# A convolution and an MLP on one core: five first-product blocks placed ahead of second products behind octet blocks, and five forward-1 blocks moved to even half steps

## The chip, the cores and the metric

The kernel runs on one core of a Trainium2 chip. The metric is the device time of one execution in microseconds. Five engines matter: TensorE (PE, matrix products; PEld is its weight load), VectorE (DVE), ScalarE (ACT), GpSimd (POOL) and SyncE (SP, which here only issues DMAs). Each engine works through its own queue in the order in which the program was written, and they wait for each other by semaphores.

## What is computed

Cut to what matters (x is `A_q`, 2048 rows of 448; F is 1792):

```python
xn = layernorm(x)
k_shift = sum of four shifted copies of k, each times its tap     # depthwise conv, 4 taps
kv = k_shift * v
y = causal convolution of kv with ssm_k over 2048 rows, by FFT    # per channel
y = y + kv * ssm_D
h = xn @ w1 + b1
out = x + xn * y + (h * tanh(softplus(h))) @ w2
```

## The kernel before, in words

The MLP is the spine. The 2048 rows are 8 chunks of 256, and the 1792 hidden columns are 14 blocks of 128, taken two at a time: 7 pairs per chunk, 56 pairs in all, numbered i. The loop at the end of `tile_kernel` runs over half steps s, two for each pair. Function `mlp_slot` says what a half step holds:

- even half step s = 2i: the first product of pair i (`g1_mm`, 22 matmuls of 256 columns, line L555), which is h for 256 columns of w1, held as a high and a low part;
- odd half step s = 2i + 1: Mish of pair i (`mish`: ACT activations L563, ACT cast of the high part `ach` L97, DVE subtraction for the low part `acl` L98), and then the second product of pair i - 2 (`g2_mm`, 12 matmuls of 448 columns, lines L587 to L589).

A chunk's second products gather in two PSUM tiles (`pg2`, one for each half of 128 rows). The pool has two buffers, so the next chunk's first second product can't begin until DVE has added both to the rows of x (`g2_evac`, line L594, output `qt`). For chunk c this addition is written at the head of the even half step behind the chunk's last second product; for chunk 2 alone (`EVAC_SOON`) it stands directly behind that product.

The convolution is hung into the same loop by two tables of work per half step, `plan` (ahead of the MLP's part, filled by `at`) and `plan2` (behind it, filled by `after`). Its stages:

- Half steps up to 62: forward-1 blocks. Each of 8 groups of the filter (`h`, half steps `H_AT`) and 8 groups of kv (half steps `KV_AT`) gets one block `f1_mm` (L165) of tiles of 32 rows by 64 columns, written to PSUM tiles `pq` and `pr`. `f1_fold` empties them: ACT copies one (L171), DVE adds and subtracts (L175) into a staging tile `st` with two buffers. `f1_out` (L186) sends `st` to DRAM (`Dh`, `Dkv`), from ACT's queue for all that matters here. Ahead of a kv block stand its taps (`taps`, DVE lines L208, L211, L213, L218, L221, result `x`; one of the four taps is multiplied by POOL, L201). If a block stands at half step t and the one before it at t - d, tap u is written behind half step t - 2 - d + d * u / 4, rounded down.
- Half steps 66 to 87, every third: octets (`octet`): inverse-1 of the octet before (`i1_mm`, L309), then two forward-2 blocks (`f2_mm`, L254), of the filter part `ah` and of the kv part `av`, loaded from DRAM by `o_load` (L238, L241). Even half steps hold an octet and then a first product; odd ones hold an octet and then a second product. The first product behind an odd octet goes to PSUM bank `pa`, which the octet itself has used.
- After half step 92: inverse-2 and the gate.

So at an odd half step with a forward-1 block, PE's row is first product, forward-1, second product, first product; at an even one it is second product, forward-1, first product, second product.

Of the kernel before, what the change touches and what calls it, by code (L numbers as in the profile page):

```python
# [20 lines left out]
NO = 8  # L21
# [1 line left out]

G2_LAG = 2
H_HEAD = 1
H_AT = {2: 6, 3: 9, 0: 12, 4: 16, 5: 20, 6: 26, 7: 32}
KV_AT = (24, 29, 34, 39, 44, 50, 55, 59)
POOL_H = {20: (0, 2)}
OCT_AT = (66, 3)
I2_AT = {100: ((6, 7, 0, 1), 92, (95, 97, 98, 99), (0, 2, 0, 1)),  # L30
# [9 lines left out]
NT_HOW[5] = dict(NT_AT, q=-8, stats=-4, flush=-2)  # L40
NT_STATS = {3: 27, 4: 41, 5: 53, 6: 70, 7: 82}
EVAC_SOON = 2,
END = 288
HEAD = (D, D, 192 + NF, 512, 2 * D, 512)
WARM_N = (448, 448, 448)
# [4 lines left out]
def tile_kernel(ctx: ExitStack, tc, q, qT, k, v, sk, hT, sD, head, w1, w2, c_g, c_gi, c_i2, out):  # L50
# [24 lines left out]
    Dh = dp.tile([NO * 16, 32, D], F32, name="Dh")  # L75
    Dkv = dp.tile([NO * 16, 32, D], F32, name="Dkv")
# [19 lines left out]
    def split(h, l, raw):  # L96
        nc.scalar.copy(h, raw)  # L97
        V.tensor_sub(l, raw, h)  # L98
# [7 lines left out]
    def bank(n):  # L106
        return bk(duo[n // 2], n % 2)

    def pg():
        return g1p[0].tile([128, 512], F32, name="pg1")  # L110
# [9 lines left out]
    def dv(n=1):  # L120
        for _ in range(n):
            if drip:
                drip.pop(0)()
# [4 lines left out]
    def at(slot, fn, *args):  # L128
        plan.setdefault(int(slot), []).append((fn, args))
# [97 lines left out]
    GT, AH, AV, HS, Y = {}, {}, {}, {}, {}  # L227
# [172 lines left out]
    def w1_hi(p, a=0, b=256):  # L400
        nc.scalar.copy(w1h[:, :, 256 * p + a:256 * p + b], w1_raw(p, a, b))

    def w1_lo(p, a=0, b=256, eng=V):
        fs, rw = slice(256 * p + a, 256 * p + b), w1_raw(p, a, b)
        V.tensor_sub(w1l[:, :, fs], rw[:, 0:3], w1h[:, 0:3, fs])
        eng.tensor_sub(w1h[64:128, 3, fs], rw[64:128, 3], w1h[64:128, 3, fs])
# [128 lines left out]
    def g1_mm(i):  # L535
        c, p = pairs[i]
        XH, XL = XS[c]
        pt = [(bank(GB[i]) if i in GB else pg()).rearrange("p (a b) -> p a b", a=2) for _ in range(2 if i == 0 else 1)]
        ps = [pt[n % len(pt)][:, n] for n in range(2)]
        mm = [[], []]  # L540
        for n in range(2):
            f = 2 * p + n
            fs = slice(128 * f, 128 * f + 128)
            hh, hl, lh = ([(w[:, kt, fs], x[:, kt]) for kt in range(3)] for w, x in ((w1h, XH), (w1h, XL), (w1l, XH)))
            th, tl = ((w1h[:, 3, fs], x[:, 3]) for x in (XH, XL))
            mm[n] = [(n, *m) for m in hh + lh + [th] + hl + [tl]]

            if 0 < i < NP:
                mm[n] = [(n, *m) for m in hh + hl + lh + [th, tl]]
        if i == 0:  # L550
            seq = mm[0][:7] + mm[1][:3] + mm[0][7:] + mm[1][7:10] + mm[1][3:7] + mm[1][10:]
        else:
            seq = mm[0] + mm[1]
        for n_, (n, l, r) in enumerate(seq):
            nc.tensor.matmul(ps[n], l, r, start=all(m[0] != n for m in seq[:n_]), stop=all(m[0] != n for m in seq[n_ + 1:]))  # L555
        P1[i] = ps

    def mish(i):
        p = pairs[i][1]
        ps = P1.pop(i)  # L560
        a = mp.tile([128, 2, CH], F32, name="a", bufs=2)
        for n in range(2):
            nc.scalar.activation(a[:, n], ps[n], AF.Mish, bias=b1t[:, 2 * p + n:2 * p + n + 1])  # L563
            if i == n == 0:
                w1_hi(2)
        if i == 0:
            w1_lo(2)
        ah = mp.tile([128, 2, CH], F32R, name="ach", bufs=3)
        al = mp.tile([128, 2, CH], F32R, name="acl", bufs=3)
        AHL[i] = ah, al  # L570
        if 2 * i + 1 in hv:
            held.append(lambda: split(ah, al, a))
        else:
            split(ah, al, a)
            dv()
# [15 lines left out]
    def g2_evac(c, jjs=(0, 1)):  # L591
        x = Q[c]
        for jj in jjs:
            V.tensor_add(x[:, jj], P2.pop((c, jj))[:, :D], x[:, jj])  # L594
            dv()
            if late(c):
                nc.sync.dma_start(out[:, 2 * c + jj], x[:, jj])

    def g2_end(j):
# [4 lines left out]
        g2_evac(c, (0,))  # L604
        for b, cs, eng in ((0, slice(0, END), nc.scalar), (2, slice(END, D), nc.sync)):
            ps = bank(b)[:, :cs.stop - cs.start]
# [9 lines left out]
    def mlp_slot(s):  # L616
        i, half = divmod(s, 2)
        n = len(pairs)
        j = i - G2_LAG
        if half == 0:  # L620
            if i < n:
                c, p = pairs[i]
                if c + 1 < NT:
                    if p == 0:
                        ln_load(c + 1)
                    if p == (3 if c in (0, 2) else 2):
                        ln_stats(c + 1)
                    if c == 0:
                        dv(len(drip))
                    if p == NP - 1:  # L630
                        ln_T(c + 1, 1)
                g1_mm(i)
        else:
            if i < n:
                c, p = pairs[i]
                if p == NP - 2 and c + 1 < NT:
                    ln_T(c + 1, 0)
                if s not in hv:
                    mish(i)
            if 0 <= j < n - 1:  # L640
                g2_mm(j)
                if pairs[j][1] == NP - 1 and pairs[j][0] in EVAC_SOON:
                    g2_evac(pairs[j][0])
            elif j == n - 1:
                g2_end(j)
# [4 lines left out]

    for g, t in H_AT.items():
        if g != H_HEAD:
# [10 lines left out]
    for g in range(-2, 0):  # L663
        at(12, k_load, g)
    for g, t in enumerate(KV_AT):
        d = t - (KV_AT[g - 1] if g else t - 6)
        at(t - d - (3 if g > 1 else 2), k_load, g)
        at(t - d - 1, v_load, g)
        for u in range(4):
            after(t - (2 if g else 1) - d + d * u / 4, taps, g, u)  # L670
        at(t, f1_mm, KV, g, "kv")
        if g + 1 < NO:
            after(t, taps_pool, g + 1, 2)
        after(t, f1_fold, g, "kv")
        (at if t % 2 else after)(t + (3 if g < NO - 1 else 2), f1_out, Dkv, g, "kv")

    for p in range(NP):
        if p >= 3:
# [11 lines left out]
    for o in range(NO):  # L690
        s, d = OCT_AT[0] + OCT_AT[1] * o, OCT_AT[1]
        ib, hb, vb = ((0, 1), (2, 0), (1, 2)) if s % 2 == 0 else ((0, 2), (1, 0), (2, 1))
        (at if o else after)(s - d if o else s - 7, o_load, AH, Dh, o, "ah")
        at(s - d - 1 if o else s - 3, o_load, AV, Dkv, o, "av")
        at(s, octet, o, ib, hb, vb)
        at(s, gi_load, o)
        after(s, prod, o)
        if s % 2:
            hv.add(s)
            GB[s // 2 + 1] = 0  # L700
        else:
            GB[s // 2], GB[s // 2 + 1] = 0, 2
# [100 lines left out]
    for s in range(nslots):  # L803
        j = s // 2 - G2_LAG - 1
        if s % 2 == 0 and j >= 0 and pairs[j][1] == NP - 1 and pairs[j][0] not in EVAC_SOON:
            g2_evac(pairs[j][0])
# [85 lines left out]
```

## Time and profile before

| what | value |
|---|---|
| median of 3 runs | 356.9 us (356.87 to 358.35) |
| the profiled execution | 357.13 us, of which the span from first to last instruction is 355.4 |
| granted TensorE clock, mean | 0.999 |
| DVE busy | 282.8 us, 80% of the span |
| ACT, POOL busy | 160.4 us (45%), 73.7 us (21%) |

The page's second part cuts the span into 40 slices of 8.9 us, a digit for each: the busy share in tenths. The row of DVE:

```profile
DVE  5999658998999998997539868868985963788943
```

DVE is nearly full from about 62 to 160 us (the eighth digit to the eighteenth): there the taps and folds of the kv blocks lie.

### The profile page before, as it was taken

What the parts mean: (1) busy time and instruction counts of PE and PEld (TensorE: products, weight loads), DVE (VectorE), ACT (ScalarE), POOL (GpSimd) and SP (SyncE); (2) the same over time, 40 slices, a digit from 0 to 9 for tenths busy, and PEclk for the clock granted to TensorE, in tenths of its full rate; (3) what the DMA queues carried; (4) which work ended last, traced back from release to release, by engine and by line L of the source; (5) the groups of instructions that cost most, each with busy time, mean ns of one, the idle gap of its engine ahead of it and who ended that gap; (6) DMA issues with size and microseconds to landing.
All of it is one profiled execution on the core that took longest, in us unless ns stands there. A gap on an engine that the chain in (4) does not pass through costs nothing.

```text
span 355.4 us, 7520 instructions
## 1 busy us (share of the span) xinstructions
PE 351.0 (99%) x3098; PEld 290.2 (82%) x3098; DVE 282.8 (80%) x375; ACT 160.4 (45%) x310; POOL 73.7 (21%) x85
## 2 busy tenths in 40 slices
PE   8999999999999999999999999999999999999996
PEld 3988888888888989888987568658757799979795
DVE  5999658998999998997539868868985963788943
ACT  4966552347343643373232732233634333354480
POOL 3047002822220250222000120110310116040030
PEclk9999999999999999999999999999999999999999
DMA  7999977949769347664869489679755466989176
GB/s 262 370 328 321 410 291 175 344 121 245 207 182 315 126 149 177 216 162 110 245 198 352 122 310 314 224 237 378 252 183 210 105 170 258 406 332 277 28 116 144
DMA packets 30835, 83.27 MB, mean 234 GB/s; under 512 B 3153, under 2 KB 15954, under 8 KB 30802
## 3 DMA queue, kind: packets, MB, share of 16 engines
q1 hardware_dynamic: 21986, 47.78, 39.5%
q0 software_dynamic: 4928, 22.95, 20.7%
q10 hardware_dynamic: 3888, 12.08, 13.1%
q8 instruction: 24, 0.39, 0.4%
q14 instruction: 9, 0.07, 0.1%
HBM read 54.34 MB, written 28.45 MB: 233 GB/s over the span
## 4 chain that ended last, share of the span: by engine, by line
PE 99%; DVE 0%; issue 0%
PE pg L555 24%; PE pg L587 13%; PE pg L589 13%; PE pg L588 12%; PE pa L555 6%; PE pq L555 5%; PE pq L165 4%; PE pa L309 3%; PE pr L555 3%; PE pq L254 3%; PE pr L254 3%; PE pp L555 2%; PE pa L254 1%; PE pg L743 1%; PE pp L363 1%; PE pg L507 1%
## 5 line engine op out<-in xcount | busy, mean ns | idle before, releaser
L587 PE MATMUL pg<-w2h,ach 128*128 128x448 f32 x222 | 81.7, 368 | 0.0
L589 PE MATMUL pg<-w2h,acl 128*128 128x448 f32 x222 | 80.7, 364 | 0.0
L588 PE MATMUL pg<-w2l,ach 128*128 128x448 f32 x222 | 80.5, 363 | 0.0
L98 DVE TENSOR_TENSOR acl<-a,ach 128x512 fp32r<-128x512 f32 x56 | 38.9, 695 | 34.3 <-ACT ach L97 34.2
L555 PE MATMUL pg<-XH,w1h 128*128 128x256 f32 x264 | 52.7, 283 | 0.0
L563 ACT ACTIVATE a<-pg,b1t 128x256 f32<-128x256 f32 x66 | 27.8, 471 | 54.3 <-PE pg L555 43.4
L587 PEld LDWEIGHTS pg<-w2h,ach 128*128 128x128 f32 x222 | 41.6, 188 | 9.4 <-issue 5.0
L555 PEld LDWEIGHTS pg<-XH,w1h 128*128 128x128 f32 x264 | 41.5, 188 | 6.8 <-issue 4.2
L589 PEld LDWEIGHTS pg<-w2h,acl 128*128 128x128 f32 x222 | 41.7, 188 | 2.5
L588 PEld LDWEIGHTS pg<-w2l,ach 128*128 128x128 f32 x222 | 41.8, 188 | 2.3
L555 PE MATMUL pg<-XL,w1h 128*128 128x256 f32 x264 | 43.0, 278 | 0.0
L175 DVE TENSOR_TENSOR st<-pq,st 128x896 f32<-128x896 f32 x32 | 34.8, 1089 | 4.7 <-ACT st L171 3.8
L555 PEld LDWEIGHTS pg<-XL,w1h 128*128 128x128 f32 x264 | 36.0, 188 | 0.0
L97 ACT CAST ach<-a 128x512 fp32r<-128x512 f32 x56 | 34.8, 621 | 1.7
L555 PE MATMUL pg<-XH,w1l 128*128 128x256 f32 x198 | 33.6, 279 | 0.0
L201 POOL TENSOR_TENSOR x<-kr,skb 128x896 f32<-128x896 f32 x8 | 17.0, 2128 | 70.5 <-PE pr L165 26.3
L320 POOL DMA_DIRECT2D E<-qe x14 | 8.8, 630 | 94.4 <-ACT qe L263 94.4
L218 DVE TENSOR_TENSOR x<-x 128x896 f32<-128x896 f32 x24 | 26.2, 1092 | 2.0 <-POOL x L201 1.4
L555 PEld LDWEIGHTS pg<-XH,w1l 128*128 128x128 f32 x198 | 27.7, 189 | 0.0
L171 ACT COPY st<-pr 128x896 f32<-128x896 f32 x16 | 14.5, 906 | 13.5 <-PE pr L165 10.7
L563 ACT ACTIVATE a<-pa,b1t 128x256 f32<-128x256 f32 x16 | 6.7, 471 | 30.5 <-PE pa L555 30.5
L165 PE MATMUL pr<-x,con 32*64 32x448 f32 x128 | 15.9, 560 | 0.0
(191 smaller groups left out, 649.2 us busy)
## 6 DMA issues: line engine op xcount, KB each, us to landing
Dkv<-st ACTq DMA_DIRECT2D x16, 448.0 KB, 5.2
ah<-Dh SPq DMA_DIRECT2D x8, 896.0 KB, 7.6
av<-Dkv SPq DMA_DIRECT2D x8, 896.0 KB, 9.5
e<-E POOLq DMA_DIRECT2D x8, 896.0 KB, 7.3
E<-qe POOLq DMA_DIRECT2D x14, 448.0 KB, 7.2
kr<-in_k_dram SPq DMA_DIRECT2D x10, 448.0 KB, 5.9
Dh<-st ACTq DMA_DIRECT2D x10, 448.0 KB, 6.8
x<-in_v_dram SPq DMA_DIRECT2D x8, 448.0 KB, 6.2
```

Of the source, the lines that this page charges most:

```text
L97: nc.scalar.copy(h, raw)
L98: V.tensor_sub(l, raw, h)
L165: nc.tensor.matmul(ps[h][64 * jj:64 * jj + 64, b, :D], f1[rg:rg + 32], x[rg:rg + 32, jj], start=True, stop=True, tile_position=(rg, 64 * jj))
L175: f(st[:, n], e, st[:, 1])
L201: nc.gpsimd.tensor_mul(o, KR[g - u // 2], skb[:, u:u + 1].to_broadcast([128, 2, D]))
L218: V.tensor_add(KV[g], KV[g], o)
L254: nc.tensor.matmul(bk(p, r)[32 * t:32 * t + 32, :D], g[rs, t, c], a[rs, t], start=True, stop=True, tile_position=(64 * r, 32 * t))
L555: nc.tensor.matmul(ps[n], l, r, start=all(m[0] != n for m in seq[:n_]), stop=all(m[0] != n for m in seq[n_ + 1:]))
L563: nc.scalar.activation(a[:, n], ps[n], AF.Mish, bias=b1t[:, 2 * p + n:2 * p + n + 1])
L587: nc.tensor.matmul(ps, ah[:, n, cs], w2h[:, f], start=f == 0, stop=False)
L588: nc.tensor.matmul(ps, ah[:, n, cs], w2l[:, f], start=False, stop=False)
L589: nc.tensor.matmul(ps, al[:, n, cs], w2h[:, f], start=False, stop=f == NF - 1 or (f == NF - 3 and jj == 1 and c == NCHUNK - 1))
```

## The change

The diff, all of it:

```diff
-H_AT = {2: 6, 3: 9, 0: 12, 4: 16, 5: 20, 6: 26, 7: 32}
-KV_AT = (24, 29, 34, 39, 44, 50, 55, 59)
+H_AT = {2: 6, 3: 10, 0: 12, 4: 16, 5: 20, 6: 26, 7: 32}
+KV_AT = (24, 30, 34, 40, 44, 50, 56, 60)
...
+G1_SOON = (69, 75, 81, 87, 89)
...
-                g1_mm(i)
+                if s - 1 not in G1_SOON:
+                    g1_mm(i)
...
                 if s not in hv:
                     mish(i)
+            if s in G1_SOON:
+                g1_mm(i + 1)
             if 0 <= j < n - 1:
                 g2_mm(j)
...
-        (at if t % 2 else after)(t + (3 if g < NO - 1 else 2), f1_out, Dkv, g, "kv")
+        (after if g < NO - 1 else at)(t + (3 if g < NO - 1 else 2), f1_out, Dkv, g, "kv")
...
-        (at if o else after)(s - d if o else s - 7, o_load, AH, Dh, o, "ah")
+        (at if o else after)(s - d if o else s - 6, o_load, AH, Dh, o, "ah")
```

It has two halves. First, at the odd half steps 69, 75, 81 and 87 (octets 1, 3, 5 and 7) and at 89 (the last inverse-1) the next pair's first product is written ahead of the second product, and is left out of the even half step behind. Second, the forward-1 blocks at 9, 29, 39, 55 and 59 go to 10, 30, 40, 56 and 60; their taps, folds and stores go with them. The distances d between kv blocks, which were 5, 5, 5, 5, 6, 5, 4, become 6, 4, 6, 4, 6, 6, 4. The first load of `ah` moves one half step later. Line numbers from 43 to 631 are one higher in the changed kernel: L98 before is L99 after, L594 is L595, L165 is L166. No instruction is added or taken away on any engine but for semaphore work.

**First place: PE around kv block 1, at half step 29 before and 30 now** (the four other blocks that move look the same). Before, from the last matmuls of pair 14's first product to the second product behind the block:

```order
L555 MATMUL pg_1052<-XL,w1h 128x256 x4
L165 MATMUL pq<-x,con 64x448 x2
L165 MATMUL pr<-x,con 64x448 x2
L165 MATMUL pq<-x,con 64x448 x2
L165 MATMUL pr<-x,con 64x448 x2
L587 MATMUL pg_753<-w2h,ach 128x448
```

And in the changed kernel, from the last matmul of the second product to the first product behind the block:

```order
L590 MATMUL pg_757<-w2h,acl 128x448
L166 MATMUL pq<-x,con 64x448 x2
L166 MATMUL pr<-x,con 64x448 x2
L166 MATMUL pq<-x,con 64x448 x2
L166 MATMUL pr<-x,con 64x448 x2
L556 MATMUL pg_1108<-XH,w1h 128x256 x3
```

The block has gone behind one second product (12 matmuls); a first product now follows it where a second product did.

**Second place: DVE between half steps 29 and 32.** Here stand the second half of the taps of kv block 2 (half step 34 in both kernels), the fold of kv block 1, and at the end the emptying of chunk 1's second products (`qt`). Before, from the low half of pair 14's Mish on:

```order
L98 TENSOR_TENSOR acl<-a,ach 128x512
L200 MEMSET x 1x1
L175 TENSOR_TENSOR st<-pq,st 128x896 x2
L218 TENSOR_TENSOR x<-x 128x896
L211 TENSOR_TENSOR x<-kr,skb 128x448
L213 TENSOR_TENSOR x<-kr,skb 128x448
L218 TENSOR_TENSOR x<-x 128x896
L221 TENSOR_TENSOR x<-x 128x896
L98 TENSOR_TENSOR acl<-a,ach 128x512
L594 TENSOR_TENSOR qt<-pg_753,qt 128x448
L594 TENSOR_TENSOR qt<-pg_757,qt 128x448
```

And in the changed kernel, directly behind the same low half of pair 14 (its own row is left out here):

```order
L212 TENSOR_TENSOR x<-kr,skb 128x448
L214 TENSOR_TENSOR x<-kr,skb 128x448
L219 TENSOR_TENSOR x<-x 128x896
L201 MEMSET x 1x1
L176 TENSOR_TENSOR st<-pq,st 128x896 x2
L219 TENSOR_TENSOR x<-x 128x896
L99 TENSOR_TENSOR acl<-a,ach 128x512
L212 TENSOR_TENSOR x<-kr,skb 128x448
L214 TENSOR_TENSOR x<-kr,skb 128x448
L219 TENSOR_TENSOR x<-x 128x896
L222 TENSOR_TENSOR x<-x 128x896
L595 TENSOR_TENSOR qt<-pg_753,qt 128x448
```

Three instructions of tap 1 (L212, L214 and the sum L219) stood ahead of that low half before and now stand behind it, so they lie between it and `qt`. Pair 15's low half still stands ahead of `qt`.

**Third place: PE behind the octet of half step 69.** Before, from the end of forward-2:

```order
L254 MATMUL pb<-ah,g 32x448
L254 MATMUL pr<-av,g 32x448 x8
L254 MATMUL pq<-av,g 32x448 x8
L587 MATMUL pg_2053<-w2h,ach 128x448
L588 MATMUL pg_2053<-w2l,ach 128x448
L589 MATMUL pg_2053<-w2h,acl 128x448
```

And in the changed kernel:

```order
L255 MATMUL pb<-ah,g 32x448
L255 MATMUL pr<-av,g 32x448 x8
L255 MATMUL pq<-av,g 32x448 x8
L556 MATMUL pa<-XH,w1h 128x256 x3
L556 MATMUL pa<-XH,w1l 128x256 x3
L556 MATMUL pa<-XH,w1h 128x256
```

The first product of pair 35 has moved ahead of the second product of pair 32; behind it two second products stand in a row.

## The prediction

> **What bounds the kernel now.** I read the page's busy times first and then its chain of waits:
>
> ```profile
> PE 351.0 (99%) x3098; PEld 290.2 (82%) x3098; DVE 282.8 (80%) x375; ACT 160.4 (45%) x310; POOL 73.7 (21%) x85
> ...
> PE 99%; DVE 0%; issue 0%
> ```
>
> PE is busy for 99% of the span and the chain that ended last runs on PE alone. The change adds and removes no matmul. So it can gain only the few hundredths of a microsecond that PE loses where one kind of block follows another, and it can lose whatever PE comes to wait for. I take the two apart: first PE's own pace, then the queues that the moved work is put into. Base is the profiled execution, 357.13 us, its span of 355.4 and 1.73 around it; it lies 0.23 us above the median of 356.9.
>
> **PE's pace around a forward-1 block.** The timeline of PE, first row of each block (start, duration, then the tile), gives block times as differences of starts:
>
> ```profile
> 97.46 0.36 PE L587 MATMUL pg<-w2h,ach 128*128 128x448 f32 x1
> ...
> 99.96 0.59 PE L165 MATMUL pq<-x,con 32*64 32x448 f32 x2
> ...
> 100.89 0.62 PE L555 MATMUL pg<-XH,w1h 128*128 128x256 f32 x3
> ...
> 103.52 0.36 PE L587 MATMUL pg<-w2h,ach 128*128 128x448 f32 x1
> ...
> 105.92 0.52 PE L555 MATMUL pg<-XH,w1h 128*128 128x256 f32 x3
> ...
> 108.42 0.36 PE L587 MATMUL pg<-w2h,ach 128*128 128x448 f32 x1
> ...
> 110.83 0.51 PE L555 MATMUL pg<-XH,w1h 128*128 128x256 f32 x3
> ...
> 113.42 0.59 PE L165 MATMUL pq<-x,con 32*64 32x448 f32 x2
> ...
> 114.36 0.47 PE L587 MATMUL pg<-w2h,ach 128*128 128x448 f32 x1
> ...
> 116.88 0.52 PE L555 MATMUL pg<-XH,w1h 128*128 128x256 f32 x3
> ...
> 119.47 0.37 PE L587 MATMUL pg<-w2h,ach 128*128 128x448 f32 x1
> ```
>
> Undisturbed, a second product takes 2.40 us (103.52 to 105.92) and a first product 2.50 (105.92 to 108.42). Around the even block at 99.96 the second product takes 2.50, the block 0.93 and the first product 2.63: 6.06 for the three. With one undisturbed first product (2.50) that is 8.56. The odd block at 113.42 holds the same four blocks, first product, forward-1, second product, first product, from 110.83 to 119.47: 8.64. What is dearer is the last one: the first product behind the second product takes 2.59 instead of 2.50, though nothing in the row says that it waits. So an odd place costs 0.08 us more than an even one. Five blocks move: **-0.40 us**, and each needs this pace to return behind one first product, as it does at 105.92.
>
> [...]
>
> **PE's pace behind an octet.** The same view behind four octets; each pair of rows bounds a first product:
>
> ```profile
> 203.89 0.51 PE L555 MATMUL pa<-XH,w1h 128*128 128x256 f32 x3
> ...
> 206.39 0.36 PE L587 MATMUL pg<-w2h,ach 128*128 128x448 f32 x1
> ...
> 213.81 0.62 PE L555 MATMUL pa<-XH,w1h 128*128 128x256 f32 x3
> ...
> 216.42 0.36 PE L587 MATMUL pg<-w2h,ach 128*128 128x448 f32 x1
> ...
> 226.34 0.47 PE L587 MATMUL pg<-w2h,ach 128*128 128x448 f32 x1
> ...
> 228.86 0.52 PE L555 MATMUL pa<-XH,w1h 128*128 128x256 f32 x3
> ...
> 231.45 0.37 PE L587 MATMUL pg<-w2h,ach 128*128 128x448 f32 x1
> ...
> 238.87 0.62 PE L555 MATMUL pa<-XH,w1h 128*128 128x256 f32 x3
> ...
> 241.56 0.37 PE L587 MATMUL pg<-w2h,ach 128*128 128x448 f32 x1
> ```
>
> Behind the odd octet before 226.34, second and first product take 5.11 together. With the first product ahead, as behind the even octets, it is 2.61 (213.81) or 2.69 (238.87) plus 2.40: 5.01 or 5.09. So the new order gains 0.02 to 0.10 at octets 3, 5 and 7, and nothing at octet 1, where the first product already takes 2.50 (203.89). At half step 89 a block edge is only traded for another. I take **-0.15 us** for this half, between 0 and -0.30. Waits are not added: `pa` is emptied by ACT while the two forward-2 blocks of `av` still run, exactly as it is at an even octet, where the first product follows at once.
>
> **DVE's queue ahead of half step 33.** This is the part that costs. The timeline of DVE, from tap 1 of kv block 2 on:
>
> ```profile
> 84.89 0.62 DVE L211 TENSOR_TENSOR x<-kr,skb 128x448 f32<-128x448 f32 x1
> 85.42 0.62 DVE L213 TENSOR_TENSOR x<-kr,skb 128x448 f32<-128x448 f32 x1
> 86.07 1.09 DVE L218 TENSOR_TENSOR x<-x 128x896 f32<-128x896 f32 x1
> 88.37 0.69 DVE L98 TENSOR_TENSOR acl<-a,ach 128x512 fp32r<-128x512 f32 x1 [1.21 <-ACT ach L97]
> ...
> 96.33 1.15 DVE L594 TENSOR_TENSOR qt<-pg,qt 128x448 f32<-128x448 f32 x2
> 97.39 2.21 DVE L175 TENSOR_TENSOR st<-pq,st 128x896 f32<-128x896 f32 x2
> ```
>
> The low half `acl` at 88.37 is the last point at which DVE waits, 1.21 us for ACT's cast; from there to `qt` at 96.33 it is busy with next to no gap. In the changed kernel the three tap instructions of the first rows stand behind that `acl` instead of ahead of it: 84.89 to 87.16, 2.2 us net of the overlap. They can't use the idle 1.21 us, since the queue is in order and ACT's row ahead of that cast is not moved. `qt` therefore begins at about 96.33 + 2.2 = 98.53, and its first half (two of them in 1.15 us, 0.62 each by their overlap) ends at 99.15.
>
> The second product that begins at 97.46 is the first of chunk 2. It writes the PSUM tile that `qt` frees. Before, it found it free with 97.46 - 96.95 = 0.51 us to spare. Two blocks are moved ahead of this point, so it would begin at 97.30; now it waits until 99.15: **+1.85 us**. The fold of filter block 7 stands behind `qt` and ends 2.2 later than before, at 97.39 + 2.21 + 2.2 = 101.80; forward-1 of kv block 2, at 99.96 before, needs the PSUM that it frees, and would start at 99.80 + 1.85 = 101.65: another **+0.15 us**. Together 2.0. Queued behind the waiting matmul on PE is everything; no later stage has idle PE time to give it back.
>
> **Three places with little left.** The kv blocks now come in steps of 4 as well as 6, and the last one later:
>
> ```profile
> 26.49 1.08 DVE L98 TENSOR_TENSOR w2l<-kr,w2h 128x896 fp32r<-128x896 f32 x1
> ...
> 124.58 1.09 DVE L221 TENSOR_TENSOR x<-x 128x896 f32<-128x896 f32 x1
> ...
> 165.74 1.09 DVE L221 TENSOR_TENSOR x<-x 128x896 f32<-128x896 f32 x1
> ```
>
> ```profile
> 126.90 0.59 PE L165 MATMUL pq<-x,con 32*64 32x448 f32 x2
> ...
> 167.30 0.59 PE L165 MATMUL pq<-x,con 32*64 32x448 f32 x2
> ```
>
> Block 4's last tap ended at 125.67, 1.23 us ahead of its matmuls. DVE's row up to there is some 2.2 late in the changed kernel plus one `acl` (0.69) that now stands ahead, against PE's 2.0 less three moves: 0.3 to 0.5 is left. Block 7's ended at 166.83, 0.47 ahead; its step stays 4 and one `acl` comes ahead there too, so about nothing is left. The low part of w2 that the second product of half step 9 needs ends at 27.57; that product loses the 0.94 us of the block ahead of it and needs it at 27.6: nothing, or 0.1.
>
> The third place is a chain of DMAs. The store of `st` and the load of `av` for octet 0:
>
> ```profile
> 171.99 1.24 ACTq L186 DMA_DIRECT2D Dkv<-st  x2
> ...
> 179.58 0.37 SPq L241 DMA_DIRECT2D av<-Dkv  x1
> ...
> 186.84 0.15 PEld L254 LDWEIGHTS pq<-av,g 64*32 64x32 f32 x8 [0.22 <-issue]
> ```
>
> ```profile
> DMA to landing us min/median/max: 4.1/6.7/10.9
> ...
> DMA to landing us min/median/max: 4.9/9.5/10.9
> ```
>
> The two last rows are those of all `Dkv` DMAs and of all `av` loads. Octet 0's load is issued when block 7's second store has landed and is itself, alone in its stretch, at the minimum of 4.9 (184.5), 2.3 us ahead of the first weights from it at 186.84. Block 7's move puts this chain 2.4 us (a second product) later against the octet: about -0.1 is left. With the median of 9.5 it would be 4.7 us late. The staging tile is a second such chain: kv block 1's store is now written behind half step 33, one half step later in step with its block and one more by `after`, and the fold of block 2 needs that buffer; at 6.7 to landing this just fits, at 10.9 it holds DVE up by 4 and PE by about 3.5. I take **+0.25 us** for all of this, nearest to the rows as they stand, with 0 and 4.7 as ends.
>
> **The sum.** -0.40 - 0.15 + 2.0 + 0.25 = +1.7 us: 358.8 for the profiled execution, **358.6 us** against the median. Its own range, from the ends of the small terms, is 357.9 to 359.4.
>
> **The rivals.**
>
> *DVE is not late at chunk 2 (not slower).* The place is the same `qt`. If the added 2.2 us found cover, that is if `acl` of pair 14 came 1.85 us earlier, the second product at half step 33 would wait for nothing, and neither would the fold. Then only the gains stay: -0.40 - 0.15, and 0 for the rest: 356.9 - 0.55 = 356.3. It decides at 97.30, the time by which the first `qt` must end. For it: DVE idles 1.21 us just ahead. Against it: that idle ends with ACT's cast, and the added rows stand behind it; 7.96 us of DVE work (88.37 to 96.33) with next to no gap follow. 14 in 100.
>
> *The DMAs are late as well (slower).* If the stores of `st` or the load of `av` take what their views show as usual or worst and not the quick landings of the rows quoted, block 4 or octet 0 waits 1 to 4 us more: about 360.1. For it: 9.5 is the median of the eight loads. Against it: the slow loads share their time with others, and the first was quick. [...] 22 in 100.
>
> *The pace doesn't depend on the order.* If the slow first product is not tied to the odd place, the -0.40 and -0.15 go: 356.9 + 2.25 = 359.2. For it: behind the even octet at 238.87 a first product is slow too. Against it: at even forward-1 blocks it is quick. [...] 9 in 100.
>
> **How the numbers follow.** The forecast has 52 in 100, and 3 are left for what I don't see. A measurement of this kernel can tell about 0.5%, 1.8 us, from no change; that line is at 358.7. The forecast's own range is cut by it: 29 of its 52 within, 23 slower. Of the first rival 12 are within and 2 faster; the second's 22 are slower; of the third 8 are slower and 1 within; of the last 3, 2 are within and 1 faster. Faster 0.03, same 0.44, slower 0.53. The range that holds the time 8 in 10 leaves out the upper half of the second rival and reaches down to the first: 356.2 to 360.3.
>
> **What would show it.** In the changed profile PE should stand still for 1.5 to 2.2 us ahead of the second product at about 97 us, with DVE's `qt` as what it waits for, and briefly ahead of the next forward-1 block. The first products behind the five moved blocks should take 2.63 and the ones after 2.50. Behind the odd octets first and second product should take 5.0 to 5.1. The forecast is wrong if PE has no gap at 97 us, if it has one ahead of the weights from `av`, or if it has one at block 4 or 7 above 0.5.

## The result, and the profile after

| what | before | after |
|---|---|---|
| median | 357.73 us (6 runs, 356.87 to 358.35) | 360.0 us (6 runs, 359.5 to 361.41) |
| ratio | | 1.0078, 95% interval 1.006 to 1.0096 |
| the profiled execution | 357.13 us, span 355.4 | 360.51 us, span 358.6 |
| mean granted clock, by run | 0.999 in the profile | 0.995, 1.0, 0.993, 1.0, 0.995, 1.0 |

The change costs 2.3 us, more than the 0.5% that can be told from none. The forecast was 358.6 us: 1.7 us on top of 356.9, the median of three runs of the kernel before. Six runs of it have 357.73, so 0.83 of the 1.4 us between 358.6 and 360.0 lies in the base, and 0.57 in the change. Direction and place were right; the cost was larger.

The page of the changed kernel, its busy times, its clock row in 40 slices of 9.0 us and its chain:

```profile
PE 352.2 (98%) x3098; PEld 289.7 (81%) x3098; DVE 282.4 (79%) x375; ACT 160.9 (45%) x310; POOL 72.3 (20%) x85
...
PEclk9999999999989999999999999999999999999999
...
PE 91%; DVE 3%; issue 2%; POOL 1%; DMA 1%; ACT 0%; ACTq 0%; POOLq 0%
```

The chain was PE alone before; now it runs through DVE for 3%. The clock row has one 8, in the twelfth slice (about 99 to 108 us). The timeline of PE there (start, duration, engine, line, operation, and in brackets the idle time ahead and what ended it):

```profile
94.81 0.62 PE L556 MATMUL pg<-XH,w1h 128*128 128x256 f32 x3
...
99.46 0.47 PE L588 MATMUL pg<-w2h,ach 128*128 128x448 f32 x1 [1.86 <-DVE qt L595]
99.77 0.36 PE L589 MATMUL pg<-w2l,ach 128*128 128x448 f32 x1
...
100.78 0.57 PE L590 MATMUL pg<-w2h,acl 128*128 128x448 f32 x1
...
103.52 0.69 PE L166 MATMUL pq<-x,con 32*64 32x448 f32 x2
...
104.53 0.62 PE L556 MATMUL pg<-XH,w1h 128*128 128x256 f32 x3
```

The first product of 94.81 should be over after 2.63, as it was before the change; the second product begins after 4.65. That is 2.02 us of standing still, and `qt` ends it, as forecast. What follows was not forecast: the second product takes 4.06 us (99.46 to 103.52) in place of 2.50, with no wait inside it. From 100.4 its matmuls take 0.57 us in place of 0.36. The forward-1 block behind it, from 103.52, takes 1.01 in place of 0.93, again with no wait in its row. The same stretch in windows (busy us of PE, PEld, DVE, ACT and POOL, then the granted clock, the DMAs' share and GB/s):

```profile
97.30:99.40 2.10, 0.30 (x3) 0.10 (x1) 2.07 (x4) 1.46 (x3) 0.00 (x0) 1.00 0.02 3
99.40:101.50 2.10, 2.04 (x7) 1.85 (x8) 2.06 (x4) 0.00 (x0) 0.00 (x0) 0.72 0.82 167
101.50:103.50 2.00, 2.00 (x6) 1.32 (x4) 2.00 (x3) 0.00 (x0) 0.00 (x0) 0.50 1.00 235
103.50:105.00 1.50, 1.50 (x21) 0.77 (x21) 1.47 (x4) 0.00 (x0) 0.00 (x0) 0.91 0.90 294
```

**TensorE's clock is halved behind the gap**, for about 3.4 us that begin some 0.9 us after work has resumed: a mean clock of 0.72 over 2.10 us means 1.18 us at half clock, 0.91 over 1.50 us means 0.27, so it lasts from about 100.3 to 103.8. In this execution that costs 4.06 - 2.50 = 1.56 us in the second product and 0.08 in the block behind it.

The timeline of DVE, where it waits between 61 and 132 us, `qt`, and the fold of filter block 7:

```profile
76.06 0.69 DVE L99 TENSOR_TENSOR acl<-a,ach 128x512 fp32r<-128x512 f32 x1 [0.55 <-ACT ach L98]
...
78.61 0.69 DVE L518 TENSOR_TENSOR XL<-pg,XH 128x512 fp32r<-128x512 f32 x1 [0.86 <-ACT XH L520]
...
88.69 0.69 DVE L99 TENSOR_TENSOR acl<-a,ach 128x512 fp32r<-128x512 f32 x1 [2.13 <-ACT ach L98]
...
98.79 1.15 DVE L595 TENSOR_TENSOR qt<-pg,qt 128x448 f32<-128x448 f32 x2
99.85 2.20 DVE L176 TENSOR_TENSOR st<-pq,st 128x896 f32<-128x896 f32 x2
```

By these rows DVE now idles 0.55 + 0.86 + 2.13 = 3.54 us ahead of `qt`. Before, it was 1.37: the 1.21 at 88.37, and 0.16 in this row of the timeline before:

```profile
75.03 1.09 DVE L218 TENSOR_TENSOR x<-x 128x896 f32<-128x896 f32 x1 [0.16 <-POOL x L201]
```

`qt` comes 2.46 us later (98.79 for 96.33): 0.32 us at the `acl` of 88 us, 2.14 behind it. Nearly all of that is idle time: from 61 us to `qt`, short pauses included, DVE is busy for 33.62 of 37.79 us now and was for 33.48 of 35.33, so it idles 2.32 us more.

Three further rows of the changed kernel's timelines, of PEld at half step 9, and of PE around kv block 3 and behind the odd octet 1:

```profile
27.54 0.19 PEld L589 LDWEIGHTS pg<-w2l,ach 128*128 128x128 f32 x1 [0.32 <-DVE w2l L99]
```

```profile
116.96 0.36 PE L588 MATMUL pg<-w2h,ach 128*128 128x448 f32 x1
...
119.46 0.59 PE L166 MATMUL pq<-x,con 32*64 32x448 f32 x2
...
120.40 0.62 PE L556 MATMUL pg<-XH,w1h 128*128 128x256 f32 x3
...
123.02 0.36 PE L588 MATMUL pg<-w2h,ach 128*128 128x448 f32 x1
...
125.42 0.52 PE L556 MATMUL pg<-XH,w1h 128*128 128x256 f32 x3
...
127.93 0.36 PE L588 MATMUL pg<-w2h,ach 128*128 128x448 f32 x1
...
204.70 0.62 PE L556 MATMUL pa<-XH,w1h 128*128 128x256 f32 x3
...
207.40 0.37 PE L588 MATMUL pg<-w2h,ach 128*128 128x448 f32 x1
...
209.81 0.36 PE L588 MATMUL pg<-w2h,ach 128*128 128x448 f32 x1
```

The wait for `w2l` is 0.32 us. The moved block 3 takes 2.50 + 0.94 + 2.62 and the next first product is back at 2.50 (125.42 to 127.93). The octet's first two products take 5.11 (204.70 to 209.81); before, they took 5.02 (201.37 to 206.39).

### The profile page after: what moved, and what is told of

It is laid out like the page before. It is cut to its first block, busy times and chain, and to the rows that moved or that the text cites. A ratio compares the mean times of both kernels' runs of the same rounds, so it can differ in the third digit from the quotient of the medians.

```text
span 358.6 us, 7527 instructions
## 1 busy us (share of the span) xinstructions
PE 352.2 (98%) x3098; PEld 289.7 (81%) x3098; DVE 282.4 (79%) x375; ACT 160.9 (45%) x310; POOL 72.3 (20%) x85
## 4 chain that ended last, share of the span: by engine, by line
PE 91%; DVE 3%; issue 2%; POOL 1%; DMA 1%; ACT 0%; ACTq 0%; POOLq 0%
PE pg L556 21%; PE pg L590 12%; PE pg L589 12%; PE pg L588 12%; PE pa L556 6%; PE pq L556 5%; PE pq L166 3%; PE pa L310 3%; PE pr L556 3%; PE pq L255 3%; PE pr L255 3%; PE pp L556 2%; PE pa L255 1%; PE pg L508 1%; PE pp L364 1%
## 5 line engine op out<-in xcount | busy, mean ns | idle before, releaser
L99 DVE TENSOR_TENSOR acl<-a,ach 128x512 fp32r<-128x512 f32 x56 | 38.9, 695 | 34.8 <-ACT ach L98 34.6
L98 ACT CAST ach<-a 128x512 fp32r<-128x512 f32 x56 | 34.8, 621 | 8.2 <-PE pg L589 6.7
L219 DVE TENSOR_TENSOR x<-x 128x896 f32<-128x896 f32 x24 | 26.2, 1090 | 0.9
L166 PE MATMUL pq<-x,con 32*64 32x448 f32 x128 | 16.0, 562 | 0.0
```

The lines of the kernel that those rows point to most:

```text
L166: nc.tensor.matmul(ps[h][64 * jj:64 * jj + 64, b, :D], f1[rg:rg + 32], x[rg:rg + 32, jj], start=True, stop=True, tile_position=(rg, 64 * jj))
L219: V.tensor_add(KV[g], KV[g], o)
```

## The experiments

The theory after this reading: all the loss is DVE's lateness at one place, plus the clock that falls behind the gap. Each run below was timed beside the kernel before; ratios are to it.

### One move undone, the gap filled with work, the gap padded, and the wait for w2l undone

`e1_undo29`, the changed kernel with kv block 1 back in its old place:

```diff
-KV_AT = (24, 30, 34, 40, 44, 50, 56, 60)
+KV_AT = (24, 29, 34, 40, 44, 50, 56, 60)
-        (after if g < NO - 1 else at)(t + (3 if g < NO - 1 else 2), f1_out, Dkv, g, "kv")
+        (after if g < NO - 1 and t % 2 == 0 else at)(t + (3 if g < NO - 1 else 2), f1_out, Dkv, g, "kv")
```

> The changed kernel with one of its five moves undone: the forward-1 product of kv block 1 stands at half step 29 again, with its output store where it was. Theory (the whole loss comes from DVE being late at the second product of half step 33, and the low clock is a result of that gap): no gap of PE over 0.2 us waiting for qt there, granted clock 1.0 through 95 to 105 us and in the profiled run, and a time of before +0.31 (w2l wait at half step 9) -0.30 (three other moved blocks) -0.13 (octets) = before -0.1, ratio 0.9997, within 0.998 to 1.001. Rival 1 (the low clock comes by itself, not from the gap): mean clocks of 0.993 to 0.995 in about half of the runs, ratio 1.001 to 1.004. Rival 2 (the octet half or the other moved blocks cost): still over 1 us above before, ratio 1.003 or more.

Measured: 357.16 us, ratio 0.9995 (0.9982 to 1.0008), no wait of PE for `qt`, clocks of 0.998 and more in all 12 runs. The four other moves and the octet half together cost nothing; **the whole loss hangs on kv block 1**.

`e2_pair17_first`, due work put into the gap:

```diff
-G1_SOON = (69, 75, 81, 87, 89)
+G1_SOON = (33, 69, 75, 81, 87, 89)
```

> The changed kernel, and the first product of pair 17 is issued ahead of the second product of half step 33 (33 added to the list of such half steps): 2.5 us of work that is due anyway stands in the place of the gap. Theory: DVE is as late as in the changed kernel, but PE does not stand still: gap for qt under 0.3 us, clock 1.0 in that stretch, the first product behind it is gone from half step 34, and the time is that of the undone move, before -0.1 (ratio 0.998 to 1.001), less than the changed kernel by 2.0 us and more. Rival (DVE's lateness is only passed on, to the evacuation behind it or to the forward-1 of kv block 2): the gap stands at a later place, 1 us or more of it, and the ratio is 1.003 or more.

Measured: 361.2 us, ratio 1.01 (1.007 to 1.0129). The theory missed, the rival is right. The timeline of PE, first rows of pair 17's first product and of the second product, and the next row with a wait for DVE:

```profile
97.50 0.50 PE L556 MATMUL pg<-XH,w1h 128*128 128x256 f32 x3
...
100.00 0.36 PE L588 MATMUL pg<-w2h,ach 128*128 128x448 f32 x1
...
128.93 0.59 PE L166 MATMUL pq<-x,con 32*64 32x448 f32 x2 [2.02 <-DVE x L222]
```

No wait at 100.00, and the 2 us come back ahead of kv block 4's forward-1. DVE's rows from 95 to 127 us stand within 0.12 us of the changed kernel's: DVE is busy throughout, and PE may run ahead of it, but meets it again. Four of the six runs have a mean clock of 0.994 or 0.995. The profiled one is at 1.0, so that the clock fell behind that later gap is likely, but not shown.

`e3_padded_gap`, 18 matmuls without use in the gap:

```diff
+            if s == 33:
+                pad_mm(i + 1, 18)
             if 0 <= j < n - 1:
                 g2_mm(j)
...
+    def pad_mm(i, n):
+        c, p = pairs[i]
+        PAD[i] = pt = pg()
+        for k in range(n):
+            nc.tensor.matmul(pt[:, :CH], w1h[:, k % 4, 256 * p:256 * p + 128], XS[c][0][:, k % 4], start=True, stop=True)
```

> [...] Theory (the low clock follows from standing still): second product begins at 99.4 to 99.6 us as in the changed kernel and lasts 2.5 us in place of 4.07; all five runs and the profile have a granted clock of 1.0; spans as in those runs of the changed kernel with a mean clock of 1.0 (357.5 to 358.1), so before +2.0, ratio 1.005 to 1.006. Rival (the low clock has nothing to do with the gap, or is a matter of the work at that place): clock 0.5 for 3 us there again in about half of the runs, ratio 1.007 to 1.010.

Measured: 359.94 us, ratio 1.0072 (1.0053 to 1.0091), clocks of 0.999 and 1.0 in all six runs. The 18 matmuls fill the gap whole, from 98.20 to 100.25; the second product begins 2.05 us late, about as before, and takes 2.60. Its windows from the padding on (columns as above):

```profile
98.20:100.20 2.00, 2.00 (x20) 2.00 (x19) 1.97 (x4) 1.47 (x3) 0.00 (x0) 1.00 0.05 13
100.20:102.20 2.00, 2.00 (x12) 1.86 (x12) 1.97 (x3) 0.00 (x0) 0.00 (x0) 1.00 0.84 172
```

DVE and the DMAs do there what they did in the changed kernel, and the clock stays at 1.00. That speaks for PE's standing still as what sets the fall off; alone, none of six runs against three of six could be chance, and the widths below have to bear it out. The median is no better, though: its spans are 357.6 to 358.7, those of the changed kernel at full clock 357.5 to 358.1 and with the low clock 358.0 to 359.5. The padding cures the clock, not the wait.

`e4_w2l_undone`:

```diff
-H_AT = {2: 6, 3: 10, 0: 12, 4: 16, 5: 20, 6: 26, 7: 32}
+H_AT = {2: 6, 3: 9, 0: 12, 4: 16, 5: 20, 6: 26, 7: 32}
```

> The changed kernel with filter block 3's forward-1 back at half step 9: the place where the second product of half step 9 waited 0.32 us for w2l. Theory: that wait goes (under 0.05 us), the gap for qt at half step 33 stays at 1.9 to 2.2 us, and the time is the changed kernel's less 0.2 to 0.3 us: ratio 1.005 to 1.009 against before. Rival (the wait for w2l only ran beside something else that sets the end): the wait goes and the block starts behind half step 12 are unchanged within 0.1 us.

Measured: 361.02 us, ratio 1.0095 (1.0073 to 1.0117). Inconclusive for what it was made for: the wait at half step 9 is gone, but in the profiled run another of 0.4 us for `w2l` came one second product later, since a load of w1 landed later there (ACT's cast waits 2.92 us for it, 2.19 in the changed kernel), and five of six runs had the low clock. The gap at half step 33 stood, at 1.82 us.

### How wide a gap has to be

The kernel before, with operations without use ahead of `qt` on DVE (n = 3, 4 and 6), and nothing else changed:

```diff
+    def late_dve(n):
+        for _ in range(n):
+            V.bn_stats(mp.tile([128, 2, 6], F32, name="bst", bufs=2)[:, 0], Q[1][:, 0])
+
+    after(31, late_dve, 3)
```

> The kernel before, with three statistics operations without use (128x448, about 0.55 us each, their result is not read) on DVE ahead of the evacuation of chunk 1: a gap of a chosen width at the second product of half step 33, and nothing else moved. That product has 0.5 us to spare in the kernel before. Theory: gap of 1.0 to 1.3 us, nothing of it made up later (DVE is busy throughout), time before +1.0 to +1.4, ratio 1.003 to 1.004. Clock, if it falls only behind gaps of about 2 us: 1.0 in all runs. Rival (any gap can set it off): below 0.996 in some runs.

> The same with four such operations: gap of 1.6 to 1.9 us, time before +1.6 to +2.0 with clock 1.0 in all runs (ratio 1.0045 to 1.0055) if a gap of this width is still short of what sets the clock off; if it is as good as the changed kernel's 2.06 us, a clock of 0.993 to 0.995 in some runs and there 1 to 1.5 us more.

> The same with six such operations: gap of 2.7 to 3.0 us. If the clock falls behind a gap by its width: 0.993 to 0.995 in most runs, 0.5 for 3 us or more behind the gap in the profile, time before +4 to +4.5 there (ratio 1.011 to 1.0125). If the changed kernel's low clock has another cause than the gap: clock 1.0, before +2.7 to +3.1 (ratio 1.0075 to 1.0085).

Measured: 358.69 us (ratio 1.0038, 1.0024 to 1.0053), 359.44 (1.0061, 1.0044 to 1.0078) and 361.65 (1.011, 1.0088 to 1.0131). The rows of the waiting matmul in the three timelines of PE:

```profile
98.87 0.47 PE L587 MATMUL pg<-w2h,ach 128*128 128x448 f32 x1 [1.16 <-DVE qt L594]
```

```profile
99.41 0.48 PE L587 MATMUL pg<-w2h,ach 128*128 128x448 f32 x1 [1.68 <-DVE qt L594]
```

```profile
100.40 0.48 PE L587 MATMUL pg<-w2h,ach 128*128 128x448 f32 x1 [2.73 <-DVE qt L594]
```

And the windows of the widest, behind its gap:

```profile
100.40:101.50 1.10, 1.10 (x5) 1.04 (x6) 1.10 (x2) 0.00 (x0) 0.00 (x0) 1.00 0.00 0
101.50:103.50 2.00, 2.00 (x7) 1.77 (x7) 1.97 (x3) 0.00 (x0) 0.00 (x0) 0.54 0.56 229
103.50:105.50 2.00, 2.00 (x19) 0.41 (x18) 2.00 (x4) 0.00 (x0) 0.00 (x0) 0.61 0.00 0
```

The same halving, made in the kernel before by the gap alone. All kernels of this study by their widest wait around half step 33 or ahead of kv block 4, each width from one profiled run, with the runs that had a mean clock of 0.995 or less:

| idle ahead, from the row | kernels | runs with the low clock |
|---|---|---|
| 0 to 0.2 us, or padded | e1, e3, e8, e9, e11 | 0 of 54 |
| 0.46, 1.16, 1.42, 1.53, 1.68 | e5, g3, e10, e7, g4 | 0 of 36 |
| 1.82, 1.86, 1.93, 2.02, 2.73 | e4, after, e6, e2, g6 | 5 of 6, 3 of 6, 4 of 10, 4 of 6, 4 of 6 |

Of the profiles themselves only two show the fall, those of the changed kernel and of g6; e2, e4 and e6 were profiled at full clock, behind gaps just as wide. So a gap of this width brings it in some executions, not in all. Within one kernel the mean span with the low clock is 0.9 (after), 1.5 (e4), 1.7 (g6), 1.7 (e6) or 2.6 us (e2) above that at full clock, from one to six runs on each side. One run of the kernel before had 0.994, in 79 beside these experiments, so something else can do it too, but seldom.

### What makes DVE late

`e5_taps_early`, the changed kernel with the taps of kv blocks 1 and 2 released at their old half steps:

```diff
-            after(t - (2 if g else 1) - d + d * u / 4, taps, g, u)
+            b, e = {1: (29, 5), 2: (34, 5)}.get(g, (t, d))
+            after(b - (2 if g else 1) - e + e * u / 4, taps, g, u)
```

> The changed kernel, with the taps of kv blocks 1 and 2 (DVE's share of the short filters) released at the half steps of the kernel before, their forward-1 products where the change put them. In the changed kernel DVE stands idle for 0.55, 0.86 and 2.13 us at 76 to 89 us (before: 0.16 and 1.21), because block 1's taps are spread over six half steps in place of five; from 89 to 135 us it runs without a pause in both. Theory A (DVE has no time to spare in that stretch, and all idle time it gains there comes out as a wait of PE somewhere): the idle time at 76 to 79 goes, but the later folds of the products move it to another place of DVE; PE's waits are split, 0.6 to 1.1 us at half step 33 and as much ahead of forward-1 of kv block 4 at about 129 us, 1.6 to 2.4 us together; time before +1.5 to +2.3 (ratio 1.004 to 1.0065), and since no single gap reaches 1.5 us all clocks are 1.0. Theory B (only the taps' release costs): PE waits under 0.3 us at either place, time before -0.1, ratio 0.998 to 1.001. Theory C (it is the product's place on PE): the gap stays 1.9 to 2.2 us at half step 33 with clocks of 0.993 to 0.995 in some runs.

Measured: 358.07 us, ratio 1.0024 (1.001 to 1.0038), all clocks 0.998 and more. None of the three hit: one gap of 0.46 us by its row (the product ahead of it lasts 0.62 us longer than without) at half step 33, and no wait ahead of block 4. PE also waits 0.77 us for `w2l` at half step 9, which is part of this run's loss. DVE's idle time was back at 0.17 and 1.26. What was left of the gap is an oversight of the edit: GpSimd's tap of block 2 was still released behind half step 30, too late to be used, so DVE multiplied it as well. DVE's groups between 60 and 200 us show one such multiplication more than the kernel before (L208 there, 7):

```profile
L209 DVE TENSOR_TENSOR x<-kr,skb 128x896 f32<-128x896 f32 x8 | 8.7, 1082 | 0.0
```

1.08 us of work against 0.51 us to spare comes to 0.57 us, near the 0.62 of the gap.

`e6_late_taps_alone`, the other way round: the kernel before, every product in place, with only those taps as late as in the change:

```diff
-            after(t - (2 if g else 1) - d + d * u / 4, taps, g, u)
+            b, e = {1: (30, 6), 2: (34, 4)}.get(g, (t, d))
+            after(b - (2 if g else 1) - e + e * u / 4, taps, g, u)
```

> The kernel before, every product on TensorE where it stood, with only the taps of kv blocks 1 and 2 on DVE released at the half steps that the change gives them (block 1 spread over six half steps, block 2 over four). If the taps' release is what makes DVE late: DVE idle 0.5, 0.8 and 2.1 us at 76 to 89 us as in the changed kernel, a gap of 1.9 to 2.3 us for qt at half step 33, clocks of 0.993 to 0.995 in some of the runs, time before +2.1 to +3.6 (ratio 1.006 to 1.010). If the place of block 1's product and fold is what counts: no gap over 0.3 us, ratio 0.999 to 1.001.

Measured: 360.64 us, ratio 1.0073 (1.0052 to 1.0095). One of its eleven runs took 894.92 us, for a reason that is not known; it counts in the median alone. The row of DVE's longest idle time, that of the waiting matmul, and that of the forward-1 block behind:

```profile
88.31 0.69 DVE L98 TENSOR_TENSOR acl<-a,ach 128x512 fp32r<-128x512 f32 x1 [2.12 <-ACT ach L97]
```

```profile
99.23 0.47 PE L587 MATMUL pg<-w2h,ach 128*128 128x448 f32 x1 [1.93 <-DVE qt L594]
...
101.89 0.59 PE L165 MATMUL pq<-x,con 32*64 32x448 f32 x2
```

**The late taps alone make the whole loss**, without a product being moved.

`e7_taps_reordered`, the changed kernel with the old releases, GpSimd's part among them, and block 2's fourth tap ahead of its third (`taps` has got a flag for the last of a block, here and in the two runs behind):

```diff
+            b, e = {1: (29, 5), 2: (34, 5)}.get(g, (t, d))
+            w = (0, 1, 3, 2)[u] if g == 2 else u
+            after(b - (2 if g else 1) - e + e * u / 4, taps, g, w, u == 3)
...
-            after(t, taps_pool, g + 1, 2)
+            after(29 if g == 1 else t, taps_pool, g + 1, 2)
```

> The changed kernel, all five products where the change put them, the taps of kv blocks 1 and 2 released as in the kernel before, block 2's fourth tap ahead of its third, and GpSimd's part of it released as before: so DVE keeps its work of the kernel before (the run with early taps had one multiplication of 1.08 us more, since GpSimd's part came too late to be used, and a gap of 0.62 us). Theory (DVE's idle time and its amount of work set the gap): no gap over 0.2 us at half step 33, at most 1.1 us of wait ahead of kv block 4's forward-1 at 127 to 130 us, clocks 1.0, time before -0.1 to +0.9 (ratio 0.9997 to 1.0025). Rival (the later fold of block 1 costs DVE as much in any order): waits of 1.6 us and more together, ratio 1.0045 or more.

Measured: 359.37 us, ratio 1.0053 (1.0032 to 1.0074): no gap at half step 33, but one of 1.53 us ahead of filter block 7's forward-1 at half step 32. By the expectation the rival would be right. But the timeline of DVE holds a row that is not the fold:

```profile
89.68 0.62 DVE L212 TENSOR_TENSOR x<-kr,skb 128x448 f32<-128x448 f32 x1
...
90.22 2.55 DVE L214 TENSOR_TENSOR x<-kr,skb 128x448 f32<-128x448 f32 x1
```

And that of GpSimd, at the same time:

```profile
89.92 2.36 POOL L202 TENSOR_TENSOR x<-kr,skb 128x896 f32<-128x896 f32 x1 [0.19 <-DVE x L201]
```

A multiplication of 0.62 us takes 2.55 and ends 0.49 us behind GpSimd's. Two runs were made to tell this from the fold. `e10_beside_gpsimd` is the kernel before with that order alone:

```diff
+            if (g, u) == (2, 3):
+                continue
...
         if g + 1 < NO:
             after(t, taps_pool, g + 1, 2)
+        if g == 1:
+            after(t, taps, 2, 3, False)
```

(the third tap moves behind half step 30, and takes over the last multiplication).

> The kernel before with the same instructions on every engine and nothing moved on TensorE; on DVE alone block 2's fourth tap (multiplications of 0.62, 0.62 and an addition of 1.09 us) is written ahead of the fold of block 1 and its third behind it, so that the multiplications run beside GpSimd's multiplication at about 89 us. In the run with reordered taps one of them took 2.55 us there in place of 0.62. Theory (DVE's multiplication stands still beside GpSimd's): one of the two takes 2.3 to 2.6 us, the gap at half step 33 is 1.1 to 1.6 us, time before +1.2 to +1.7 (ratio 1.0035 to 1.005). Rival (that row was a chance of one run, and the later fold was the reason): both take 0.62 us, no gap over 0.3 us, ratio 0.999 to 1.001.

Measured: 359.17 us, ratio 1.0045 (1.003 to 1.006). Its row of DVE, and the row of PE that waits:

```profile
89.88 2.54 DVE L213 TENSOR_TENSOR x<-kr,skb 128x448 f32<-128x448 f32 x1
```

```profile
95.73 0.59 PE L165 MATMUL pq<-x,con 32*64 32x448 f32 x2 [1.42 <-DVE st L175]
```

The slow multiplication follows the place beside GpSimd: in both runs it is the one that starts 0.3 us behind GpSimd's. Only the half step of the gap was off, 32 in place of 33.

`e11_tap_ahead`, the changed kernel with all its moves, and block 2's fourth tap two half steps earlier than in the kernel before:

```diff
+            b, e = {1: (29, 5)}.get(g, (t, d))
+            due = b - (2 if g else 1) - e + e * u / 4
+            w = u
+            if g == 2:
+                w, due = (0, 1, 3, 2)[u], (27, 28, 28, 30)[u]
+            after(due, taps, g, w, u == 3)
...
+            after(29 if g == 1 else t, taps_pool, g + 1, 2)
```

> The changed kernel with all five moves, block 1's taps as in the kernel before, and block 2's fourth tap two half steps earlier, into DVE's idle time at 88 us and clear of GpSimd's multiplication. Theory (idle time of DVE and the clash with GpSimd make the gaps, not the later fold in itself): multiplications of 0.62 us, no gap over 0.2 us at half steps 32 and 33; what DVE then loses waiting for products (0.5 us and more ahead of the fold at about 107 us) shows ahead of kv block 4's forward-1 at 127 us, 0.5 to 2.0 us; time before 0 to +1.6 (ratio 1.0 to 1.0045). Rival (the fold half a step later costs DVE as much in any order): a gap of 1.5 us or more at half step 32 or 33.

Measured: **357.25 us, ratio 0.9992 (0.9981 to 1.0003)**, all clocks 0.998 and more. Its only row of PE between 90 and 131 us that waits for another engine, and DVE's longest idle time:

```profile
127.56 0.59 PE L166 MATMUL pq<-x,con 32*64 32x448 f32 x2 [0.16 <-DVE x L222]
```

```profile
105.93 2.22 DVE L176 TENSOR_TENSOR st<-pq,st 128x896 f32<-128x896 f32 x2 [1.97 <-ACT st L172]
```

So a fold half a step later costs nothing in itself. And DVE idles 1.97 us at 106 with 0.16 us of PE behind it, which ends the theory of `e5` that all idle time of DVE comes out in PE: only that ahead of the tight place, half step 33, does.

### The halves that should bring something

`e8_octets_alone`, the kernel before with the octet half only:

```diff
+G1_SOON = (69, 75, 81, 87, 89)
...
-                g1_mm(i)
+                if s - 1 not in G1_SOON:
+                    g1_mm(i)
...
+            if s in G1_SOON:
+                g1_mm(i + 1)
```

`e9_rest_of_change`, the changed kernel without the moves of kv block 1 and filter block 3:

```diff
-H_AT = {2: 6, 3: 10, 0: 12, 4: 16, 5: 20, 6: 26, 7: 32}
-KV_AT = (24, 30, 34, 40, 44, 50, 56, 60)
+H_AT = {2: 6, 3: 9, 0: 12, 4: 16, 5: 20, 6: 26, 7: 32}
+KV_AT = (24, 29, 34, 40, 44, 50, 56, 60)
-        (after if g < NO - 1 else at)(t + (3 if g < NO - 1 else 2), f1_out, Dkv, g, "kv")
+        (after if g < NO - 1 and t % 2 == 0 else at)(t + (3 if g < NO - 1 else 2), f1_out, Dkv, g, "kv")
```

> The kernel before with only the octet half of the change. Theory: five fewer changes between products of unlike shapes bring 0.13 us as in the changed kernel's trace (it gained that between the first octet and the end); ratio 0.9996, within 0.999 to 1.0005. Rival (the octets cost something that the changed kernel's trace hides): ratio 1.001 or more.

> The change without its two moves that gave a wait: the octet half and the moves of kv blocks 3, 6 and 7, with kv block 1 and filter block 3 as in the kernel before. It should be the fastest of all: 3 moves of 0.10 and the octets' 0.13, so before -0.4 us (ratio 0.9988, within 0.9975 to 1.0), no gap over 0.2 us at half steps 9 and 33, all clocks 0.997 or more. If the moves' gains are taken back by waits elsewhere: ratio 0.9995 to 1.001.

Measured: 357.44 us, ratio 0.9996 (0.9982 to 1.001), and **357.05 us, ratio 0.9987 (0.9971 to 1.0002)**, the lowest median of the study, with every forecast number hit. Neither interval leaves out 1: gains of 0.1 and 0.4 us are borne out by the block times in the traces (0.30 for the three moved blocks of e9, 0.14 for the octet half in each), not by the medians.

## Why the prediction was right and wrong

From the block starts of the two traces, each term of the sum beside what it became in the profiled execution:

| step | forecast, us | measured, us |
|---|---|---|
| five forward-1 moves | -0.40 | -0.49 |
| octet half | -0.15 | -0.12 |
| second product at half step 33 waits for `qt` | +1.85 | +2.02 |
| next forward-1 waits for the fold | +0.15 | 0 |
| places with little left | +0.25 | +0.31, all of it `w2l` |
| half clock behind the gap | not in the sum | +1.64 |
| start of the kernel (7.38 for 7.63 at the first forward-1), and 33 to 77 us | not in the sum | -0.25, +0.10 |
| sum | +1.7 | +3.2 |

- **The step that failed is the size of the term "together 2.0"**, what the lateness of `qt` costs: it came to 2.02 + 1.64 = 3.66 us in the profiled execution. The wait itself was right within 0.2 us, down to its place and its releaser. But a gap was priced at its own length, and the clock behind it at nothing. TensorE ran there at half clock (0.50 from 101.5 to 103.5 us), and three of six runs show the low mean clock. These three average 360.62 us, 2.89 above the median before; the three at full clock average 359.78, 2.05 above it and 0.35 over the forecast's step.
- The wait for the fold was sized well, but was not there in this execution: the fold ended at 102.05 (99.85 + 2.20), while the half clock held the forward-1 block back until 103.52. At full clock it is there: in e4, e5, e6, g3 and g4 the second product behind the gap lasts 2.65 or 2.66 us to the start of the block, 0.15 more than 2.50, and in e6 the block starts at 101.89, 0.05 behind the fold's end. Measured against that, the half clock costs 4.06 + 1.01 - 2.65 - 0.94 = 1.48 us.
- The cause of the lateness was right, and two runs show it both ways: late taps alone bring the gap (e6), early taps with the products moved take it away (e11, which also moves one tap further ahead). The prediction's 2.2 us of taps that come behind `acl` are 2.14 us by the rows. It left out that the `acl` itself comes 0.32 later, so that DVE's idle time ahead of it grows from 1.21 to 2.13 us.
- The 0.08 per moved block came out at about 0.10: blocks 3, 6 and 7 together 0.31 (from 104.53 to 189.01, against 100.89 to 185.68), block 1 0.08, filter block 3 0.10. The third rival, by which the order is worth nothing, is refuted for these blocks.
- The octet half was right in its sum by luck. From the end of its forward-2 to the next inverse-1, octet 1 takes 7.61 us in place of 7.52, octet 5 7.51 in place of 7.61, and octets 3 and 7 are unchanged within 0.01: -0.02 for all four, where -0.06 to -0.30 was expected of three of them. The gain lies at half step 89, which the prediction took for a mere trade: 9.11 us (285.18 to 294.29) in place of 9.22 (281.86 to 291.08). In e8 and e9 it is the same, -0.02 and -0.01 for the octets, -0.12 and -0.13 for half step 89. So behind odd octets the third rival was right.
- "Nothing, or 0.1" for `w2l` was 0.32 here, and 0.16 to 1.05 by the same row in six other profiles with filter block 3 at half step 10. It was the nearest of the places with little left, and priced too low.
- Blocks 4 and 7, the load of `av` and the store of `st` never waited in the changed kernel: the second rival did not happen. The load of `av` for octet 0 was issued at 183.94, 1.8 us ahead of octet 1's, and the first weights from it were loaded at 190.17 without a wait for a DMA. The first, no lateness at all, neither; e11 shows how it could be had.

## What to carry to other kernels

When a table moves an operation, look at everything that is timed by differences of that table: here the products could move for nothing, and the release of the work ahead of them was what cost. A wait that comes into a stretch in which TensorE never stood still can cost more than its length: here the mean clock was low in 20 of 34 runs with a wait of 1.82 to 2.73 us, and the span with it 0.9 to 2.6 us longer within one kernel. It was low in none of 36 with waits of 0.46 to 1.68 us, and in none of the six in which useless matmuls filled the gap. Before work is written into an idle slot of DVE, see what GpSimd runs at that time: beside it, a multiplication of 0.62 us took 2.55.

## What the hardware showed that was not expected

- **The clock can fall behind a gap of 1.8 us and more.** In 20 of 34 runs with one idle time of 1.82 to 2.73 us the mean clock was 0.993 to 0.995, in none of 36 with 0.46 to 1.68 us. In the changed kernel's profile it was at 0.50 from 101.5 to 103.5 us. Whether 1.7 to 1.8 us is a threshold, or only the chance grows steeply there, is open. Nor do these runs show what decides, behind gaps of the same width, which executions it falls in.
- **A multiplication of DVE took four times as long beside one of GpSimd.** Both read two tensors in SBUF; DVE's, which started 0.3 us behind GpSimd's, took 2.55 (e7) and 2.54 us (e10) in place of 0.62. GpSimd's, which itself started beside the DVE multiplication ahead of that one, took 2.36 and 2.35 in place of 2.12. The fold beside the same operation, which reads PSUM and SBUF, kept its 1.09 us (2.22 for two, from 89.17, beside GpSimd's from 89.23, in the kernel before). What makes the difference between the multiplication and the fold was not shown.
